# A new order for the first third of a recurrent-attention and gated-MLP kernel

## The chip, the core and the metric

The kernel runs on one core of a Trainium2 chip. The metric is the device time of one execution in microseconds (us). The core has five engines, each with its own queue of instructions that is worked off strictly in order: TensorE (PE, matmuls), VectorE (DVE), ScalarE (ACT), GpSimd (POOL) and SyncE (SP, which issues loads and stores). An instruction that needs another engine's result waits for a semaphore, and everything behind it in its own queue waits too.

## What is computed

The reference has two parts. A gated linear recurrence over 768 time steps, for 4 batches and 8 heads of 48 columns, gives `x`; then a gated MLP with a spatial mix over the time steps:

```python
for t in range(S):
    state = alpha[:, :, t, :, None] * state + einsum('bhd,bhde', k[:, :, t], v[:, :, t])
    y[:, :, t] = einsum('bhd,bhde->bhe', q[:, :, t], state)
x = y.transpose(0, 2, 1, 3).reshape(B, S, H * D)
h = maximum(x @ w_in, 0); u, v = h[..., :512], h[..., 512:]
v_n = (v - mean(v)) / sqrt(var(v) + 1e-6)
v_s = einsum('ts,bsd->btd', w_spatial, v_n) + b_spatial[None, :, None]
out = (u * v_s) @ w_out
```

## The kernel before

The recurrence is done in chunks of 128 steps (six per batch, 24 in all). Within a chunk the running product of alpha is built from logarithms: `ln` (ACT), cumulative sums by matmuls with triangular matrices (`half`, `cum`), then exponentials on ACT: `einv` (e to the minus sum, tile `binv`) and `eexp` (e to the sum, in the PSUM bank). `kt` = k times binv, `qt` = q times the bank; both are transposed on TensorE (`tr_k`, `tr_q`), copied out of PSUM (`ev`), multiplied to scores (`sc`), masked (`ms`, `m`) and multiplied by v (`y`). The state is carried by `upd` (TensorE), `S` and `z` (VectorE, GpSimd) and `sb` (a bf16 copy). `xe` evicts x. The first four chunks are done together (`four_chunks`), and so are the four from chunk 6 on; chunks 4 and 5 are a pair; the rest are single.

The MLP per batch: `v` and `u` project (line 1006, the helper `accumulate`, which all matmuls of the MLP go through), `ve` and `ue` evict with relu, `bn` takes mean and variance, `rs` 1/sqrt, `nm` (line 1085, tile `shift`) minus mean times that, `vn` normalizes. `vn` on ACT reads `shift`; `vn` on VectorE reads the mean itself. `s` mixes over time, `se` adds the bias, `g` gates, `o` projects out, `oe` evicts, `st` stores. The bias `b_spatial` comes by one small load, `b_sp` (line 1206), that GpSimd issues; a matmul with a row of ones, `bb` (line 1033, two halves), spreads it over the partitions, and `be` evicts that to `bsp_bc`. The weights come in float32 into two buffers `raw`, so that each 768 KB load waits for the casts (`cast`) of the load two before it; the spatial weights are then transposed (`wt`, line 1018) and copied out (`we`).

The masks and triangles that are built at the start are `maskq`, `tri`, `triq`, `one`, `ident` and `causal`.

Nothing is scheduled by the machine. A string `PLAN` holds every operation in one list, and `replay` emits them in that order, which fixes the order on each engine. A word of it is an engine's letter and the number of the operation, for TensorE with the PSUM banks that it takes and filling matmuls ahead of it:

```python
P103@6,4,5,7:512#7:424#7   # op 103 on TensorE, banks 6,4,5,7; two filling matmuls into bank 7
...
op, eng = ops[int(word[1:])], LETTERS[word[0]]
...
    warm(int(cols), int(n), kind)
...
op.emit(eng)
```

A filling matmul (`warm`, line 243) multiplies a tile of constants and its result is read by nobody.

Of the kernel before, what the change touches and what calls it, by code (L numbers as in the profile page):

```python
# [37 lines left out]
LETTERS = {"P": "PE", "D": "DVE", "A": "ACT", "G": "POOL", "S": "SP"}  # L38
# [1 line left out]


PLAN = """
D2 D0 D4 D1 G9 G11 G5 G6 D3 S56 S57 S59 S58 A60 S12 S169 S170 A61 S272 S171 D8 P62@0:512#0:512#0:512#0 P66@1 P67 P63
P70@2 P71 P74@3 P75 A68 A64 D79 G82 P91@4,5 P52@6 A69 A72 A76 G7 A78 A92 A84 A65 G88 G87 A73 A77 D85 D90 D81 D93 D53
D83 D80 P103@6,4,5,7:512#7:424#7 P94@0,1 D86 D104 D89 D106 G13 P97@6,2:192#2 D98 A95 P100@3,0 D101 A96 P117@3,6:376#1
P115@4,1 A99 G107 G14 A15 A173 D102 D109 P128@0,2 D119 D118 P174@5 A116 A122 A176 P130@6,4 S16 D132 D131 S172 A135
P175@1 A129 P120@3 P54@2 G110 G105 P136@0,4 A121 A178 A55 G111 G108 P133@6 G181 A180 A134 G184 A179 D112 A177 D138
P123@7,3 P141@2 S20 G276 G277 G278 G17 G19 G18 D124 D125 P151@6 P187@7,4 P126@3 S23 S274 S273 D185 A152 A127 G186 G183
G113 G114 D182 P190@5,6 A189 A192 A142 P144@3 D137 P139@4 D188 D191 A140 G22 G21 D153 D143 P199@6,5 P196@2,7 P162@4
A280 A145 P287@0 A163 P154@1 P160@3 A279 A288 A155 D200 D201 D198 D197 D164 P193@4 A161 P156@7 A157 A165 D194 D146  # L50
P158@5 A159 G195 P202@1,2 P203 S26 A204 A147 D166 P290@4 P37@5,7 D38 P34@3,6 G24 S275 S384 S396 G25 S503 S29 D35
P207@1 D148 D208 D36 A39 A289 P205 P281@7 P40@3,5 A206 A282 A167 G10 D42 P210@2 D149 D150 D41 S385 S386 D168 D209 S398
S397 P284@5 P223@6 P219@3 P221@1 A211 A291 A224 A285 D212 A283 A220 A213 D295 D301 A286 A292 D214 D222 D215 A216
P225@6 P233@2 P217@3 P229@7 P237@0 A218 A28 D298 G297 G27 D304 G294 P226 D227 G300 G303 P43@3,5 D45 P230 P234 D231
D235 A293 A44 P46@4,6 P306@5,1 D308 P238 P49@7,3 D50 D51 A48 A47 A307 P309@2,6 P315@1,4 P312@5,7 P249@3 P250 A310 A316
A314 A296 A311 A299 D313 D317 D239 G236 D251 P338@4,1 P332@7,5 P245@0 P246 G302 G305 D333 D339 G232 P318@7,6,3,2 G240
G228 D340 D319 A507 G33 D334 D321 D247 P253@4 P330@7,1 P254 P241@5 P242 G320 A388 A400 A30 A337 A331 A32 G322 P389@0
D255 P345@7,6 D243 D324 D347 A390 P341@4 A391 P335@5 G31 G325 D394 D327 D346 G393 P401@3 A342 A336 A402 A403 P257@1
A392 S492 S387 A258 P259@4 P356@2 S399 G404 G248 G323 G326 S491 S557 P343@0,7 D405 P351@3,5 P407@1,6 A357 D328 A344
A350 A408 D353 D352 P359@2 G252 G395 P348@7 A349 P354@3 D409 S505 S494 S506 P418@6,1 P413@5,0 D358 S493 S504 S559 S547  # L60
S545 S608 S558 S548 S546 A355 A360 D415 D420 P508@7 P366@3 P410@0 P371@2 P377@1 D411 D414 A260 A509 P375@0 D419 A495
D361 A372 A561 P262@5 P496@6 G244 G329 G406 G256 A367 A376 A510 D368 G412 A497 A498 P416@0 P421@3 A422 G514 G502 G500
D378 D379 D513 G512 A417 P264@2 P267@4 A499 A362 A380 A268 D363 D501 P426@0 P423@1 P435@3 P437@6 D381 A365 A427 A424
P433@4 A434 A438 A382 D263 D436 P269@0 D364 D265 D425 D428 D383 P518@1 P369@4 A511 A270 P562@6 P373@2 A374 A429 A549
# [18 lines left out]
S484 S490 S487 S705 S261 S475 S271 G808 P864@5 D816 P823@3 P819@1 D865 P874@4 D766 D768 A824 S714 A828 A820 A875 A767
A710 D829 P871@3 D830 D831 P887@5 P885@1 P881@4 D876 D872 D873 A877 D878 D879 P913@6 P706@2 A707 P893@3 P883@7 P897@0
A884 A886 A882 A888 P889@2 D880 P894 D895 G896 P890 P898 P905@5 P906 D891 D899 P901@2 P902 G900 P914 P909@0 P910
P917@3 D903 D892 D915 G916 D904 P926@6 P920@2 P918 S708 A927 S928 A921 S922 S711 D911 D907 D908 P923@6 G912 D919
P929@2 A930 D924 S925 S931 P935@3 D936 S937 P932@6 A933 S934 P938@3 D939 S940
"""


# [42 lines left out]
def kernel(  # L133
# [23 lines left out]
    NDS = DH // 128  # L157
# [70 lines left out]
    vn = sb("vn", 2, [128, NT, DH])  # L228
# [37 lines left out]
    ops, made = [], {}  # L266
# [788 lines left out]
    def project_v(b, tt):  # L1055
# [20 lines left out]
        def rs(_):  # L1076
# [3 lines left out]

        op(("rs", b, tt - 1), "ACT", rs,
           [("bn", b, tt - 1), ("bn", b, tt), ("vn", b - 2, tt - 1), ("vn", b - 2, tt), ("zeros", 3)])
        def nm(_):
            for x in (tt - 1, tt):
                nc.vector.tensor_scalar(
                    out=shift[n2][:, x:x + 1], in0=mvs[n2][:, x, 0:1], scalar1=rstd[n2][:, x:x + 1], scalar2=-1.0,
                    op0=ALU.mult, op1=ALU.mult)
# [188 lines left out]
```

## Time and profile before

| | us |
|---|---|
| three runs, median (lowest to highest) | 138.29 (137.82 to 139.09) |
| profiled execution, its own time | 139.19 |
| span of the program in it | 137.4 |
| alpha in use (`ln 0`), first k in use (`kt 0 1` on GpSimd, `kt 0 0` on VectorE) | 5.35, 8.07, 8.40 |
| first attention scores on TensorE (`sc 0`) | 15.44 |
| last matmuls (start, duration of seven) | 133.20, 0.98 |

Times within the profile count from the span's start. A timeline row reads: start, duration, engine, line, operation, what it writes and reads, shape, count, and in brackets the idle time ahead of it with what ended it. A row of groups reads: line, engine, operation, tiles, shape, count, then busy us, mean ns of one, idle time ahead with its releaser. A row of loads reads: tile and source, queue, count, size of one and median us from issue to landing. Consecutive matmuls overlap, so that a matmul's duration is longer than the distance to the next.

### The profile page before, as it was taken

The page shows a single profiled execution, that of the slowest core. Times are in us where ns is not written, and L with a number is a line of the kernel's source. Part 1 is how long each engine was busy: PE and PEld are TensorE (multiplying, and loading weights), DVE is VectorE, ACT ScalarE, POOL GpSimd, SP SyncE. Part 2 cuts the span into 40 slices and gives each one's busy share as a digit, 9 for nine tenths or more (in the row PEclk, how much of TensorE's full clock was granted, in tenths as well). Part 3 has the DMA queues.
Part 4 walks back from the last instruction along what each step waited for, and adds up shares of the span by engine and source line. Part 5 has one row for each costly group of instructions (what it writes and reads, how often), then busy time and mean ns, then how long its engine had stood idle before and what let it go on. Part 6 is the DMA issues. An engine that isn't in the chain of part 4 may idle for free.

```text
span 137.4 us, 5308 instructions
## 1 busy us (share of the span) xinstructions
PE 131.0 (95%) x2122; PEld 79.2 (58%) x2122; DVE 120.8 (88%) x300; ACT 108.0 (79%) x261; POOL 87.2 (63%) x146
## 2 busy tenths in 40 slices
PE   6899998999999999999999999999999999999990
PEld 3365554564646566566657666656566765565560
DVE  6259999979999999999899999997999999974871
ACT  3476998899989889999997989999965796954041
POOL 7365899967399789972079989620799842003560
PEclk9999999999999999999999999999999999999999
DMA  3999999599989796899999797899991497101055
GB/s 83 371 371 382 341 321 347 132 374 383 366 164 261 159 218 127 163 184 192 195 190 209 143 205 147 167 194 226 190 181 23 158 390 257 66 0 57 0 203 203
DMA packets 76473, 28.66 MB, mean 209 GB/s; under 512 B 63008, under 2 KB 74912, under 8 KB 76448
## 3 DMA queue, kind: packets, MB, share of 16 engines
q1 hardware_dynamic: 76416, 28.32, 78.6%
q8 instruction: 16, 0.26, 0.8%
q14 instruction: 9, 0.07, 0.2%
q0 software_dynamic: 32, 0.00, 0.0%
HBM read 23.60 MB, written 4.72 MB: 206 GB/s over the span
## 4 chain that ended last, share of the span: by engine, by line
PE 76%; ACT 6%; DVE 6%; DMA 5%; issue 3%; POOL 2%; SPq 0%; POOLq 0%; ACTq 0%
PE bank L1006 53%; DMA kc<-in_k_dram 5%; PE bank L961 3%; PE bank L945 3%; PE bank L989 3%; PE bank L417 2%; PE bank L855 2%; PE bank L899 2%; PE bank L837 2%; PE bank L933 2%; DVE vn L1097 1%; PE bank L795 1%; PE bank L772 1%; ACT uT L185 1%; DVE w_spT L181 1%
## 5 line engine op out<-in xcount | busy, mean ns | idle before, releaser
L1006 PE MATMUL bank<-w_spT,vn 128*128 128x384 bf16 x192 | 35.8, 327 | 0.3 <-DVE vn L1097 0.3
L190 POOL TENSOR_TENSOR gT<-vs,uT 128x384 bf16<-128x384 f32 x28 | 25.7, 933 | 14.3 <-DVE vs L1153 14.1
L190 POOL TENSOR_TENSOR kt<-kc,binv 128x384 bf16<-128x384 f32 x22 | 20.3, 931 | 20.3 <-ACT binv L909 15.2
L1006 PEld LDWEIGHTS <-vn 128*128 128x128 bf16 x192 | 17.4, 98 | 11.7 <-DVE vn L1097 0.7
L1006 PE MATMUL bank<-w_in,xT 128*128 128x512 bf16 x72 | 19.1, 380 | 0.2 <-ACT xT L179 0.2
L1006 PE MATMUL bank<-xT,w_in 128*128 128x384 bf16 x96 | 18.7, 326 | 0.0
L1006 PE MATMUL bank<-w_out_sb,gT 128*128 128x384 bf16 (+1 forms) x100 | 18.4, 320 | 0.0
L1153 DVE TENSOR_TENSOR vs<-bank,bsp_bc 128x384 f32<-128x384 f32 x31 | 16.3, 550 | 2.4 <-PE bank L1006 2.3
L950 DVE TENSOR_TENSOR ptm<-bank,mask 128x512 bf16<-128x512 f32 x28 | 17.9, 683 | 0.4 <-PE bank L945 0.2
L179 ACT COPY kqT<-bank 128x512 bf16<-128x512 bf16 (+1 forms) x20 | 15.0, 792 | 3.1 <-PE bank L989 1.9
L1068 DVE BATCH_NORM_STATS2 stats<-v_sb 128x6 f32<-128x512 bf16 x24 | 16.4, 682 | 0.2
L185 ACT ACTIVATE v_sb<-bank 128x512 bf16<-128x512 f32 x20 | 11.8, 599 | 1.8 <-PE bank L1006 1.5
L185 ACT ACTIVATE uT<-bank 128x384 bf16<-128x384 f32 x27 | 12.4, 495 | 0.7 <-PE bank L1006 0.6
L1006 PEld LDWEIGHTS <-w_in 128*128 128x128 bf16 x96 | 9.0, 98 | 6.7 <-DVE ptm L950 0.3
L190 DVE TENSOR_TENSOR qt<-qc,bank 128x384 bf16<-128x384 f32 x24 | 12.6, 545 | 0.2 <-DMA qc<-in_q_dram 0.2
L1006 PEld LDWEIGHTS <-gT 128*128 128x128 bf16 x100 | 9.3, 98 | 5.8
L179 ACT CAST xT<-bank 128x384 bf16<-128x384 f32 x23 | 10.4, 482 | 1.8 <-PE bank L417 1.4
L844 DVE TENSOR_TENSOR ptm<-bank,mask 128x512 bf16<-128x512 f32 x16 | 10.4, 684 | 0.0
L1006 PEld LDWEIGHTS <-xT 128*128 128x128 bf16 x72 | 6.2, 97 | 6.2 <-ACT xT L179 1.2
L179 ACT COPY raw_w<-bank 128x384 f32<-128x384 f32 x8 | 3.8, 480 | 7.3 <-PE bank L1006 7.2
L394 DVE TENSOR_TENSOR zs<-bank,state 128x384 f32<-128x384 f32 x16 | 8.8, 549 | 0.5 <-PE bank L933 0.4
L243 PE MATMUL bank<-junk 128*128 128x512 f32 (+3 forms) x14 | 8.0, 700 | 1.1 <-DVE junk L1242 1.1
(162 smaller groups left out, 265.4 us busy)
## 6 DMA issues: line engine op xcount, KB each, us to landing
ac<-in_alpha_dram SPq DMA_DIRECT2D x14, 192.0 KB, 4.4
kc<-in_k_dram SPq DMA_DIRECT2D x14, 192.0 KB, 4.0
qc<-in_q_dram SPq DMA_DIRECT2D x14, 192.0 KB, 4.4
vc<-in_v_dram SPq DMA_DIRECT2D x14, 192.0 KB, 4.1
raw_w<-in_moe_w_spatial_dram SPq DMA_DIRECT2D x3, 768.0 KB, 8.0
out_dram<-o_sb SPq DMA_DIRECT2D x9, 192.0 KB, 2.0
ac<-in_alpha_dram SPq DMA_DIRECT2D x2, 768.0 KB, 6.8
kc<-in_k_dram SPq DMA_DIRECT2D x2, 768.0 KB, 7.6
```

The costliest lines, as they stand in the source:

```text
L179: nc.scalar.copy(out=out, in_=in_)
L185: nc.scalar.activation(out=out, in_=in_, func=AF.Relu)
L190: ENG[eng].tensor_tensor(out=out, in0=in0, in1=in1, op=ALU.mult)
L243: nc.tensor.matmul(out=banks[n][:, 0:cols].rearrange("p (a b) -> p a b", a=4), lhsT=junk, rhs=junk[:, None, 0:cols // 4].to_broadcast([128 ...
L394: lambda _: nc.vector.tensor_tensor(out=zs[i % 3], in0=tp(), in1=state[(i - 1) % 3], op=ALU.add),
L844: nc.vector.tensor_tensor(out=ptm[n2][:, ci, s], in0=banks[sl.bank].rearrange("p (hp t) -> p hp t", hp=HP), in1=mask[:, 3][:, None, :].to_ ...
L945: nc.tensor.matmul(out=pt[s][:, hp, :], lhsT=kT[rows, hp, :], rhs=qT[rows, hp, :], start=True, stop=True)
L950: nc.vector.tensor_tensor(out=ptm[n2][:, ci, s], in0=banks[sl_p[s].bank].rearrange("p (hp t) -> p hp t", hp=HP), in1=mask[:, 2][:, None, : ...
L961: nc.tensor.matmul(out=place(to, 3 * hp + (0, 1, 1, 2)[x]), lhsT=heads(vb, hp, x), rhs=ptm[n2][:, ci, x // 2, hp, :], start=(turn == 0), s ...
L1006: nc.tensor.matmul(out=ps, lhsT=lhsT, rhs=rhs, start=first and n == 0, stop=last and n == len(pairs) - 1)
L1068: nc.vector.bn_stats(out=stats[tt % 2], in_=v_sb[n2][:, tt, :])
L1153: nc.vector.tensor_tensor(out=vs[d], in0=banks[sl.bank][:, 0:TH], in1=bsp_bc[:, th, :], op=ALU.add)
```

## The change

The kernel's `PLAN` is replaced. SyncE's loads and stores keep their order. On the other engines the order is new up to a common operation, from which it is as before: on TensorE the last spatial-mix matmuls of batch 0 (`s 0 0 1 1`), on VectorE `z 7`, on ACT the exponential `einvs 10`, on GpSimd the last cast of w_out. The PSUM banks are dealt anew to the end. Some operations of the first third change engines (before to after):

| from | to | operations |
|---|---|---|
| VectorE | GpSimd | triq, vb 0 0, vb 1 1 |
| VectorE | ACT | be 0, ev_k 1 0, ev_q 1 0, ve 0 4, we 0 1, we 2 0, we 5 0 |
| ACT | VectorE | ev_k 0 0, ev_q 0 0, ev_k 2 1, ev_q 3 0, we 1 1, we 4 0, vn 0 2, vn 0 5 |
| GpSimd | ACT | vb 1 0, sb 0, sb 2, sb 6, and one cast each of w_in 0, w_spatial 2, w_out |
| ACT | GpSimd | vb 3 1, and one cast each of w_in 1, w_spatial 2, two of w_out |
| GpSimd | VectorE | kt 1 1 |

The beginnings of the queues, by names:

| engine | before | after |
|---|---|---|
| GpSimd | maskq, b_sp, tri, ident, kt 0 1, causal, kt 1 1, vb 1 0, cast | maskq, tri, triq, one, ident, causal, kt 0 1, b_sp, vb 1 1, vb 0 0, cast |
| TensorE | half 0 0, half 0 1, cum 0 1, cum 0 0, half 1 0, cum 1 0, half 1 1, cum 1 1, tr_k 0, bb 0, upd 0, tr_q 0, tr_k 1, tr_q 1, sc 0 | half 1 0, half 0 0, half 0 1, cum 0 0, cum 0 1, cum 1 0, half 1 1, cum 1 1, tr_k 0, bb 0, upd 0, tr_k 1, tr_q 0, tr_q 1, sc 0 |
| ACT | ln 0, ln 1, einv 0 1, einv 0 0, eexp 0 1, einv 1 0, einv 1 1, ebc, ev_k 0 0, vb 0 1, eexp 0 0, eexp 1 0, eexp 1 1, ev_q 0 0 | ln 0, ln 1, einv 0 0, einv 0 1, einv 1 0, eexp 0 0, einv 1 1, vb 1 0, vb 0 1, be 0, eexp 1 1, eexp 0 1, ebc, eexp 1 0, ev_k 1 0, ev_k 1 1, ev_q 0 1, ev_q 1 0 |
| VectorE (behind the zeros) | triq, kt 0 0, kt 1 0, vb 1 1, vb 0 0, ev_k 0 1, be 0, qt 0 1, qt 0 0, qt 1 0, S 0, qt 1 1 | kt 0 0, kt 1 0, kt 1 1, ev_k 0 0, ev_k 0 1, qt 1 1, qt 0 1, qt 0 0, S 0, qt 1 0 |

Filling matmuls, in columns: before 512, 512, 512 ahead of the first `half`, 512 and 424 ahead of `upd 0`, 192 ahead of `tr_k 1`, 376 ahead of `sc 0`; after 512, 512, 360 ahead of the first `half`, 416 ahead of `upd 0`, 120 ahead of `tr_q 0`, 384 ahead of `sc 0`.

The second part: `nm` is split into one operation for each of the two tiles, and emits nothing where the `vn` that follows is on VectorE. Before, 24 `shift` instructions are emitted; after, four, since `vn` is on ACT for four tiles (1 1, 1 2, 1 5, 3 0).

```diff
 PLAN = """
-D2 D0 D4 D1 G9 G11 G5 G6 D3 S56 S57 S59 S58 A60 S12 S169 S170 A61 S272 S171 D8 P62@0:512#0:512#0:512#0 P66@1 P67 P63
-P70@2 P71 P74@3 P75 A68 A64 D79 G82 P91@4,5 P52@6 A69 A72 A76 G7 A78 A92 A84 A65 G88 G87 A73 A77 D85 D90 D81 D93 D53
...
+S56 D0 S57 G9 D1 S59 D2 D4 G5 D3 S58 G8 G10 A60 S12 A61 P70@0:512#0:512#0:360#0 G6 P62@1 G7 P66@2 P63 P67 A64 P71 S171
+A68 P74@3 D79 A72 P75 G82 S172 A65 D85 A76 G11 P91@4,5 A87 D88 A84 G90 P52@6 D92 A53 D93 G81 A77 S275
...
 def replay(ops, held, warm, plan):
 
+    for word in plan.split():
+        op = ops[int(re.match("[A-Z]([0-9]+)", word).group(1))]
+        op.eng = LETTERS[word[0]]
     for word in plan.split():
...
-        def nm(_):
-            for x in (tt - 1, tt):
+        for x in (tt - 1, tt):
+            def nm(_, x=x):
+                if made[("vn", b, x)].eng == "DVE":
+                    return
                 nc.vector.tensor_scalar(
                     out=shift[n2][:, x:x + 1], in0=mvs[n2][:, x, 0:1], scalar1=rstd[n2][:, x:x + 1], scalar2=-1.0,
                     op0=ALU.mult, op1=ALU.mult)
 
-        op(("nm", b, tt - 1), "DVE", nm, [("rs", b, tt - 1), ("vn", b - 2, tt - 1), ("vn", b - 2, tt)])
-        for x in (tt - 1, tt):
+            op(("nm", b, x), "DVE", nm, [("rs", b, tt - 1), ("vn", b - 2, x)])
+
             def vnf(e, x=x):
...
-               [("rs", b, tt - 1), ("nm", b, tt - 1)] + [("s", b - 2, d, th, 1) for d in range(NDS) for th in range(2)])
+               [("rs", b, tt - 1), ("nm", b, x)] + [("s", b - 2, d, th, 1) for d in range(NDS) for th in range(2)])
```

In these excerpts G9 is maskq, G5 tri, G8 triq, G10 one, G6 ident, G7 causal, G82 kt 0 1, G11 b_sp, P91 tr_k 0, P52 bb 0, and D53 or A53 be 0.

More of the change, by code (lines that the diff above doesn't have):

```diff
@@ L48 @@
[L48 to L52, printed above, removed]
@@ L83 @@
[L83 to L87, printed above, removed]
+S56 D0 S57 G9 D1 S59 D2 D4 G5 D3 S58 G8 G10 A60 S12 A61 P70@0:512#0:512#0:360#0 G6 P62@1 G7 P66@2 P63 P67 A64 P71 S171
@@ new lines @@
+A68 P74@3 D79 A72 P75 G82 S172 A65 D85 A76 G11 P91@4,5 A87 D88 A84 G90 P52@6 D92 A53 D93 G81 A77 S275
+P103@5,6,4,7:416#7 A69 D89 A78 D83 A73 D80 P97@3,2 D104 A98 D86 S173 A99 G15 P94@1,5:120#1 D106 P100@0,3 A96 D95 A101
+G107 D102 S16 A175 P117@0,3:384#2 G14 P128@1,5 D109 P115@6,2 A105 D119 P177@4 G110 A116 D118 A129 P130@3,6 G108 A135
+D112 P120@0 S174 A180 G13 P123@5,1 D132 A121 P176@7 G186 S20 A181 D131 P141@6 A122 D124 G113 A178 P54@3 P133@2 A182
+D125 G279 P136@5,0 A111 A179 P126@1 D138 A134 G183 D187 A127 P152@2 A142 D184 G114 P189@4,1 D137 G280 A153 P192@6,7
@@ new lines @@
+P144@0 D190 A194 D191 G19 A18 D193 P139@4 D143 G17 A145 P198@6,1 G281 P201@7,2 A55 S23 P155@0 D200 A282 S277 P157@3
+D203 G185 S276 A140 P159@1 G188 D146 A156 P161@4 A158 G22 D199 A283 P195@0 P163@3 D196 A160 A147 D202 P290@6 G197 A164
+P284@0 D154 P204@7,1 A162 G21 A291 P205 D165 D148 D150 P207 G24 S26 P37@4,3 A206 P34@2,5 A208 S278 P209@7 A166 G25
+S389 A292 P212@1 D167 D149 D38 D39 D168 A210 D35 D169 P226@3 D170 A36 D211 S401 P287@7 A213 P40@5,2 A288 P220@4 D214
+A227 P222@1 A41 D42 P293@3 A215 D151 P224@2 A285 D216 D218 D219 A296 P236@5 D217 G297 A221 D225 P237 A289 D304 P240@4
@@ new lines @@
+A294 G300 D301 P232@6 A295 S509 D238 A223 G28 D307 P233 A286 P241 A27 D234 P43@3,1 G303 P309@5,7 D242 S29 P228@6 A44
+D45 G306 A310 D298 P49@1,3 P46@4,2 D311 P229 A50 G305 D51 A48 S390 P312@7,0 D47 G239 P318@3,1 S391 A314 D313 P315@2,4
+P252@5 D320 G302 A319 D316 S403 G308 A405 P253 D230 P335@2,3 G235 A317 D254 P341@6,1 A299 P248@0 D336 G231 A513 D342
+P256@5 A393 G243 D343 P321@2,4,7,6 S402 D337 P244@1 D322 A33 G30 S498 P249 D324 A323 P257 D250 P333@2,3 G325 P245 D258
+A340 P394@0 A334 S392 G32 D246 P348@4,5 A395 P344@3 G31 D327 A396 P338@1 S404 D350 P406@7 G328 A345 P260@2 D399 A339
@@ new lines @@
+S497 G398 A407 D330 P262@3 A408 D349 P359@6 S564 G409 A397 D410 A261 P346@0,4 D331 A360 P354@1,5 G251 S511 P412@2,7
+A347 D356 P362@6 A353 D355 A413 G326 G329 D414 P351@4 S500 G255 P357@1 D361 A352 P423@7,2 A358 S512 P418@4,5 G400
+P514@0 A363 D420 G247 P370@1 A263 S499 D425 A515 P415@5 G332 P375@3 A501 D416 S510 G411 P381@2 A376 D419 G259 A568
+P379@5 D424 A371 P265@4 G417 D364 A380 S566 P502@1 A516 P421@5 D372 A503 S554 P426@7 G520 A504 P267@3 D382 A427 G508
+S552 A422 G506 D383 P270@7 A505 A365 P431@5 S616 D519 G518 A384 D366 D368 P428@2 D507 A271 S565 A369 D385 D387 D266
@@ new lines @@
+P441@6 P443@7 A432 S555 D442 P439@4 A429 D367 P272@6 D268 A440 S553 D430 A444 P524@3 P373@4 A386 P569@7 D433 P377@2
+A517 S628 A273 P445@5 D388 A378 P532@0 P459@6 A434 D446 S630 A556 D525 D435 P455@2 A572 D437 D436 S617 A438 P557@3
+D374 P521@5,1 A570 P460 S567 D523 A571 G573 P447@4 A522 D461 S618 P448 G526 D533 P451@1 A558 D574 S629 A560 P456 G561
+D449 A559 P471@7 D457 A563 S619 P452 G462 D562 P536@2,4 D453 P527@0,5 S736 P576@3,6 D528 G454 P475@1 A577 D529 S724
+P472 G458 D537 P463@0 A620 S727 A632 D538 G534 P476 A578 P579@2 P464 D477 S631 G450 P621@4 D580 P530@3 A622 P539@6
@@ new lines @@
+D473 A531 G581 P583@2,1 D465 A623 P592@7,5 P633@3 A540 G478 D593 P541@0 A634 S726 D626 A575 P467@6 G625 A635 D585
+P479@7 S739 A542 G636 D584 A624 P544@1 D637 S738 G582 P588@2 D594 P468 A545 G627 P639@3,4 S791 A480 D469 G535 P595@1
+D589 A641 P586@6 D640 S725 G590 P642@2 A728 P485@7 D543 A596 G474 S737 P729@3 A587 D643 P650@1,4 A638 P645@5,0 D546
+S793 G644 P482@2 A486 A730 D651 P608@7 A740 G466 A732 D647 P600@1 A609 G591 S779 D646 P597@6 A747 G735 D652 P604@5
+G470 S792 A598 D610 P741@7 P653@4 G733 A744 S780 D599 P648@6 A547 P491@0 A654 S843 D483 D548 D550 A649 P658@4 A795
@@ new lines @@
+D549 D601 A605 P666@6 A492 D551 P751@5 A659 P494@1 S781 D752 A742 P670@4 D660 A611 G745 S794 P655@5 A667 D612 D614
+D615 A671 P602@6 S782 A743 D656 P488@4 A495 D613 A783 S487 P672@1 D657 A489 P606@5 A731 D753 P668@4 S855 A673 D746
+A661 S844 P796@0 P682@7 A607 D662 D664 D663 S845 A603 D665 P678@5 A797 P759@6 A798 P784@1 S846 D760 P683 A785 P679
+D734 A799 P686@6 G788 S856 D680 A786 P694@3 A847 D801 G802 A790 S857 D761 P687 G800 A669 P674@0 D684 A859 S858 P806@4
+D789 A787 P675 G681 D688 P695 P748@1,7 D807 G689 P803@6,5 D696 A749 P702@4 D676 G685 D804 A805 P815@0 P703 D750 G808
@@ new lines @@
+P860@6 P848@1 D704 P754@7,5 A849 G677 P763@3,2 P698@4 D755 A850 A861 G854 D816 P699 A851 G852 D764 P690@7 A862 D700
+P709@0 G863 D756 P691 P706@4 G817 D765 D692 P712@5 A707 D864 A710 G693 P766@7 S708 D853 P757@0 S711 D713 A767 P810@6,4
+G705 S484 P819@1,2 A758 P866@5,7 D812 S269 A809 G697 P768@0 S490 D820 A867 S496 D821 P869@4 G701 P771@1 S493 A762 D811
+S714 A769 P718@2 D870 S264 A868 D770 S481 P822@0 S274 P813@4 A823 D865 P872@7,6 A814 G871 P877@5,3 P721@0 D874 A772
+G818 D879 P835@6 D773 P831@3 A836 P827@1 D878 P824@6 A828 D873 A774 P880@5 D837 A825 P875@7 A832 P833@1 D826 A881
@@ new lines @@
+P829@3 A722 D876 A834 P885@5 S723 D775 D777 A838 D778 P882@1 A830 D839 D841 D840 A886 D842 P899@7 A776 P897@3 D887
+P893@5 A719 D883 P925@0 D884 P715@1 P905@2 A888 A716 P895@6 D889 D891 D890 D892 S717 P909@1 A896 A898 P901@4 A894 P906
+A900 P902 D907 P910 P917@7 D903 G908 D911 P918 P913@4 G912 P914 P926 D915 P921@1 D904 P922 D927 P929@4 D916 G928 D923
+P938@0 D919 P932@1 G924 A939 D920 P930 S940 A933 P935@0 D931 S934 S720 D936 P941@4 S937 P947@0 A942 P944@1 D948 S943
+P950@0 S949 A945 D951 S946 S952
```

34 lines of the change are left out of this document (removed).

## The prediction

> **What bounds the kernel now.** I read the page first, then the busy time of stretches, then the timelines of the first 16 us, because that is where the two orders differ most.
>
> ```profile
> span 137.4 us, 5308 instructions
> ...
> PE 131.0 (95%) x2122; PEld 79.2 (58%) x2122; DVE 120.8 (88%) x300; ACT 108.0 (79%) x261; POOL 87.2 (63%) x146
> ```
>
> TensorE is the engine with the least room. The stretches below begin at the first attention scores (15.44), at the matmul from which TensorE's order is again the old one (47.68), and end with its last matmul.
>
> ```profile
> core 0: us, PE busy (x) PEld busy (x) DVE busy (x) ACT busy (x) POOL busy (x), PEclk, DMA share, GB/s
> 15.44:47.68 32.24, 30.97 (x645) 17.82 (x645) 30.64 (x71) 29.58 (x72) 26.63 (x41) 1.00 0.95 285
> 47.68:134.20 86.52, 86.44 (x1305) 54.23 (x1302) 79.85 (x180) 68.94 (x173) 51.58 (x81) 1.00 0.72 164
> ```
>
> From 47.68 to 134.20 TensorE idles 0.08 us. So whatever the new order wins or loses up to that matmul is handed to the end one for one. In 15.44 to 47.68 its idle time is 32.24 - 30.97 = 1.27 us; that is the most that a better order can take out of this stretch. Before it TensorE waits for the first loads, and filling matmuls sit in the waits:
>
> ```profile
> 9.79 0.33 PE L1033 MATMUL bank<-b_sp_sb,ones_row 1*128 1x384 bf16 x1
> 10.05 1.84 PE L243 MATMUL bank<-junk 128*128 128x512 f32 x4
> 11.82 0.26 PE L795 MATMUL bank<-o_sb,kt 32*128 32x96 bf16 x8
> 12.33 0.78 PE L795 MATMUL bank<-o_sb,kt 32*128 32x96 bf16 x56 [0.24 <-POOL o_sb L181]
> ...
> 14.21 0.41 PE L772 MATMUL bank<-ident,qt 64*128 64x64 bf16 x16
> 14.61 0.90 PE L243 MATMUL bank<-junk 128*128 128x376 f32 x2
> 15.44 0.40 PE L837 MATMUL bank<-kqT 48*128 48x128 bf16 x8
> ```
>
> The reader is to see the first row: the matmul that spreads the bias (bb 0) is early in TensorE's queue and costs nothing at 9.79, because the bias has long landed.
>
> **The change, part by part.** *The bias load moves.* It is the one load that GpSimd issues, so an unchanged order of SyncE's loads does not cover it. GpSimd's rows before:
>
> ```profile
> 1.01 1.36 POOL L339 TENSOR_SCALAR_AFFINE_SELECT mask<-mask 32x128 bf16<-32x128 bf16 x4
> 2.32 0.67 POOL L1206 DMA_DIRECT2D b_sp_sb<-in_moe_b_spatial_dram  x1
> 3.04 0.20 POOL L322 MEMSET le_pair<- 128x128 bf16 x1
> ...
> 4.19 0.20 POOL masks.py:197 MEMSET ident<- 128x128 bf16 x1
> 4.46 0.29 POOL masks.py:199 TENSOR_SCALAR_AFFINE_SELECT ident<-ident 128x128 bf16<-128x128 bf16 x1
> 8.07 0.91 POOL L190 TENSOR_TENSOR kt<-kc,binv 128x384 bf16<-128x384 f32 x1 [3.31 <-ACT binv L741]
> 8.94 1.90 POOL L355 TENSOR_SCALAR_AFFINE_SELECT mask<-mask 64x128 bf16<-64x128 bf16 x4
> ...
> 32.93 0.21 POOL L347 MEMSET le_one<- 128x128 bf16 x1
> ...
> 33.88 0.29 POOL L348 TENSOR_SCALAR_AFFINE_SELECT mask<-mask 128x128 bf16<-128x128 bf16 x1
> ```
>
> ```profile
> 3.84 0.26 DVE L181 COPY le_quad<-le_pair 128x128 bf16<-128x128 bf16 x1 [0.19 <-POOL le_pair L328]
> ...
> 4.63 0.18 DVE L334 MEMSET lt_quad<- 32x16 uint32 x2
> ...
> 11.69 1.48 DVE L190 TENSOR_TENSOR qt<-qc,bank 128x384 bf16<-128x384 f32 x3 [0.20 <-DMA qc<-in_q_dram]
> 13.14 0.56 DVE L190 TENSOR_TENSOR state<-bank,bcq 128x384 f32<-128x384 f32 x1
> 13.61 0.54 DVE L190 TENSOR_TENSOR qt<-qc,bank 128x384 bf16<-128x384 f32 x1
> ```
>
> ```profile
> 7.50 0.87 ACT L741 ACTIVATE binv<-bank 128x384 bf16<-128x384 f32 x2 [0.57 <-PE bank L718]
> ...
> 11.17 1.24 ACT L744 ACTIVATE bank<-bank 128x384 f32<-128x384 f32 x3
> 13.48 1.56 ACT L179 COPY kqT<-bank 128x512 bf16<-128x512 bf16 x3 [1.07 <-PE bank L772]
> ...
> 19.14 0.49 ACT L179 CAST bsp_bc<-bank 128x384 bf16<-128x384 f32 x1
> ```
>
> In the new order GpSimd does, ahead of the bias load: maskq (ends 2.37), tri (3.04 to 4.19, 1.15), triq (0.97 on VectorE, 3.84 to 4.81; on GpSimd no row, I take 1.0), one (32.93 to 34.17, 1.24), ident (0.56), causal (1.90), and the first kt (0.91). The masks end at 2.37 + 1.15 + 1.0 + 1.24 + 0.56 + 1.90 = 8.2. kt 0 1 needs the second exponential binv, which ended at 8.37 and now comes after one more cumulative matmul, so about 8.6; the masks are hidden under that wait, up to a triq of 1.4 us. kt ends at 9.5, and there the bias load is issued instead of at 2.32.
>
> How long it takes to land is the price that decides:
>
> ```profile
> out_dram<-raw_w SPq DMA_DIRECT2D x2, 96.0 KB, 1.7
> b_sp_sb<-in_moe_b_spatial_dram POOLq DMA_DIRECT2D x1, 1.5 KB, 5.3
> ...
> kc<-in_k_dram SPq DMA_DIRECT2D x1, 384.0 KB, 7.8
> ```
>
> The same load took 5.3 us. The ends are 1.7 us, the quickest transfer of the trace (a store, at the end, when the DMA engines are nearly empty), and 7.8 us, a load of 384 KB (kc, pair 2) that SyncE issued in the full stretch around 8.4. I take 5.3, its own row: landing at 14.8. The Trainium skill, "DMA: Bandwidth & Descriptors", section "Anatomy of one DMA — SWDGE (gpsimd) path", gives a GpSimd-issued load about 2.0 us plus bytes / 436e3. By it the bias would land at 11.5 and the sum below would come out near 138.7. This case's row, 5.3, does not agree with it.
>
> *What stands behind it.* TensorE's order keeps bb 0 right after the first transposes, and a queue goes in order. be 0, the eviction of bb 0, moves from VectorE to ACT, ahead of three of the exponentials that qt needs. So both queues stand still until 14.8. From there, by rows:
> - bb 0 0.33, to 15.15. be 0 0.49 on ACT, to 15.7; the two exponentials for the first qts at 1.24 / 3 = 0.41 each, to 16.1 and 16.5.
> - VectorE: three qt from 16.1 at (13.14 - 11.69) / 3 = 0.48 each, to 17.6; state 0.47 (13.14 to 13.61), to 18.05; the fourth qt, to about 18.55. TensorE's update, which the state needs, is done earlier: a filling matmul of 416 columns at the rate of the 376 (0.90), to about 16.1, and 0.26 + 0.78 for the update, to 17.1.
> - TensorE: last transposes 0.41, to 18.95; the filling matmul of 384 columns, kept in the new order, 0.90; first scores at 19.85, where they were at 15.44: +4.4 us. ACT's last copy (1.56 / 3 = 0.52 after 18.95) is done at 19.5, under the filling matmul.
>
> *From the scores to 47.68.* TensorE has the same matmuls in another order, 30.97 us of them. With no idle time it reaches the common order at 19.85 + 30.97 = 50.8 (+3.1); with as much as before at +4.4. I take the middle, **+3.8 us**: VectorE (30.64) and ACT (29.58) are released less late than TensorE by their own sums, so part of the old idle time goes.
>
> *What moves between engines.* Casts, evictions, two of the normalizations and small copies trade places among VectorE, ACT and GpSimd; in that stretch each has between 1.6 and 5.6 us of 32.24 free, so I take nothing, with TensorE's 30.97 as cover. If that cover went, each would cost its own duration.
>
> *Filling matmuls.* Seven become six. Those ahead of the first cumulative sums end before alpha is there in both orders: nothing. After that 512 + 424 + 192 + 376 columns become 416 + 120 + 384, a saving that is in the chain above.
>
> *Shift instructions.*
>
> ```profile
> L1085 DVE TENSOR_SCALAR shift<-mvs,rstd 128x1 f32<-128x1 f32 x24 | 3.9, 206 | 1.0 <-ACT rstd L1079 1.0
> ```
>
> Of 24 only the four whose normalization is on ACT stay: 20 x 0.206 = 4.1 us of VectorE, most of it behind 47.68, where TensorE's 86.44 of 86.52 covers it. I take 0; without that cover, up to 4.1.
>
> *SyncE's loads.* Their order stays, but two wait for casts:
>
> ```profile
> 18.59 6.85 SPq L1048 DMA_DIRECT2D raw_w<-in_moe_w_spatial_dram  x2
> ```
>
> The second of these (its issue ends at 18.59 + 6.85 = 25.44) waits for the buffer that the casts of w_in free. When the chain is 4 us late these casts are late by up to as much, and so is everything behind in SyncE's queue. That cannot be more than the chain's own delay, and is why I don't forecast less than +3.1 in the likeliest case. The banks of the later matmuls are dealt anew; nothing taken.
>
> **Sum.** The profiled execution took 139.19 us (span 137.4): 139.19 + 3.8 = 143.0. It lies 0.9 above the median of the three runs, 138.29; against that, 138.29 + 3.8 = **142.1 us**.
>
> **Rivals.**
> 1. *TensorE falls back to half pace.* It would stand from about 9.9 to 14.8 without work. At the start of the trace the same 512-column passes of the filling matmul are 0.86 apart, later 0.43:
>
> ```profile
> 3.77 0.34 PEld L243 LDWEIGHTS bank<-junk 128*128 128x128 f32 x1 [0.52 <-issue]
> 4.63 0.26 PEld L243 LDWEIGHTS bank<-junk 128*128 128x128 f32 x1 [0.52 <-issue]
> ...
> 10.59 0.19 PEld L243 LDWEIGHTS bank<-junk 128*128 128x128 f32 x1 [0.24 <-issue]
> 11.02 0.19 PEld L243 LDWEIGHTS bank<-junk 128*128 128x128 f32 x1 [0.24 <-issue]
> ```
>
> The slow pace lasted from the start to 4.63, some 3.6 us. As much again after 14.8 costs up to half of it, 1.8 us: 143.9 us. Against it: the granted clock reads 1.00 everywhere, and no row shows TensorE after a long idle time. The Trainium skill, "TensorE: Matmul & The Clock Gate", Part 1, says that TensorE returns to half clock after an idle window of about 3.4 us; by that rule 4.9 us of idle time are enough if they cover such a window.
>
> 2. *The bias lands quickly: not slower.* For it: 1.7 us for the quickest transfer. Landing at 11.2 puts everything above 3.6 earlier: scores at 16.2 (+0.8), the common order at -0.5 to +0.8, and the time at 137.8 to 139.1, say 138.4. Against it: the load's own 5.3 us. It decides when the load lands less than about 2.9 us after issue, since 2.4 us off the +3.8 leaves +1.4, 1%. Were the bias not waited for at all, the scores would come at about 15.4 and the order win its idle time at most: 137.0.
>
> 3. *The bias lands later*, 7.8 us as the loads of that stretch: 2.5 more, 144.6 us.
>
> **How the numbers follow.** +3.8 as worked out 0.45 (its own range, a landing of 4 to 6 us and no or all of the idle time, 140.8 to 143.5); half pace on top 0.25; quick landing 0.25; late landing 0.05. A change of under 1% (1.4 us) is what a measurement of this kernel can't tell from none: slower 0.75, same 0.21, faster 0.04 (both from rival 2). The range from 138.6 to 144.8 leaves out about 0.13 of rival 2 and 0.05 above.
>
> **What would show it.** Right: the bias load starts near 9.5 on GpSimd, TensorE has a gap of about 5 us ahead of bb 0 that the bias load ended, ACT one ahead of bsp_bc, and the first scores stand near 19.9; after the common matmul the stretch to the last one is 86.5 as before. Half pace would show as passes 0.86 apart behind the gap. Wrong: a load issued or landed well before 14.8, or TensorE idle behind the common matmul.

## The result, and the profile after

| | before | after |
|---|---|---|
| median, us (lowest to highest; four runs each) | 138.27 (137.82 to 139.09) | 142.87 (142.74 to 143.03) |
| profiled execution, its own time and span, us | 139.19, 137.4 | 142.99, 141.2 |
| first scores (`sc 0`), us | 15.44 | 20.70 |
| first instruction of the common order on ACT (`einvs 10`), us | 48.51 | 52.32 |

The ratio is 1.0326, with a 95% interval of 1.0276 to 1.0376: slower by 4.6 us between the medians, 3.8 us between the two profiled executions. Ratios here leave disturbed executions out, and medians do not, so the two need not agree to the last tenth. In the changed kernel's code lines stand four lower, and six lower from the split `nm` on (bb 0 is L1037, a filling matmul L247, the scores L841, the bias load L1212).

First the place where the prediction expected the wait: GpSimd's issue of the bias load in the timeline, and that load's row among the DMA issues, whose last number is the time from issue to landing.

```profile
8.93 0.91 POOL L194 TENSOR_TENSOR kt<-kc,binv 128x384 bf16<-128x384 f32 x1 [1.15 <-ACT binv L745]
9.79 0.67 POOL L1212 DMA_DIRECT2D b_sp_sb<-in_moe_b_spatial_dram  x1
...
b_sp_sb<-in_moe_b_spatial_dram POOLq DMA_DIRECT2D x1, 1.5 KB, 4.6
```

Then the timeline of TensorE and of ACT behind it.

```profile
14.47 0.47 PE L1037 MATMUL bank<-b_sp_sb,ones_row 1*128 1x384 bf16 x1 [4.28 <-DMA b_sp_sb<-in_moe_b_spatial_dram]
14.88 1.76 PE L247 MATMUL bank<-junk 128*128 128x416 f32 x2
16.56 1.46 PE L799 MATMUL bank<-o_sb,kt 32*128 32x96 bf16 x64
...
20.70 0.40 PE L841 MATMUL bank<-kqT 48*128 48x128 bf16 x8
```

```profile
14.98 0.48 ACT L183 CAST bsp_bc<-bank 128x384 bf16<-128x384 f32 x1 [4.08 <-PE bank L1037]
15.36 0.87 ACT L748 ACTIVATE bank<-bank 128x384 f32<-128x384 f32 x2
```

The load lands near 14.4, TensorE stands for 4.28 us ahead of bb 0 and ACT for 4.08 ahead of be 0, with the exponentials behind it. The windows of that stretch (length, busy time and count for PE, PEld, which is TensorE's weight loads, DVE, ACT and POOL, then TensorE's granted clock, the DMA share and GB/s) show a second thing:

```profile
10.00:15.00 5.00, 0.72 (x10) 0.29 (x8) 2.50 (x4) 0.92 (x4) 2.03 (x4) 0.67 1.11 366
15.00:20.00 5.00, 4.90 (x117) 3.25 (x118) 3.37 (x8) 3.46 (x9) 0.25 (x1) 0.65 1.12 364
```

The granted clock fell to 0.67 and 0.65, and the filling matmul behind bb 0 took 1.76 us for 416 columns. The loads that depend on casts follow: the issue of the w_spatial loads begins 4.5 us later than before (23.11 against 18.59).

```profile
23.11 6.74 SPq L1052 DMA_DIRECT2D raw_w<-in_moe_w_spatial_dram  x2
```

From the first instruction of the common order to the end the two kernels are alike. One window of each, after first, then before:

```profile
52.32:141.20 88.88, 84.99 (x1286) 53.69 (x1294) 77.97 (x165) 68.53 (x172) 51.19 (x81) 1.00 0.71 164
```

```profile
48.51:137.40 88.89, 85.61 (x1296) 53.62 (x1290) 79.37 (x179) 68.68 (x171) 50.75 (x80) 1.00 0.72 165
```

88.88 and 88.89 us. All of the loss arises ahead of that point. (Of the profiles below, all but one need 88.8 to 89.4 us for this stretch; e3 needed 90.2.)

### The profile page after: what moved, and what is told of

It reads as the page before. It is cut to its first block, busy times and chain, and to the rows that moved or that the text cites. A ratio compares the mean times of both kernels' runs of the same rounds, so it can differ in the third digit from the quotient of the medians.

```text
span 141.2 us, 5260 instructions
## 1 busy us (share of the span) xinstructions
PE 129.6 (92%) x2106; PEld 79.6 (56%) x2120; DVE 118.1 (84%) x274; ACT 107.5 (76%) x262; POOL 86.2 (61%) x151
## 4 chain that ended last, share of the span: by engine, by line
PE 81%; DMA 7%; ACT 5%; issue 3%; DVE 1%; POOL 1%; POOLq 0%; ACTq 0%
PE bank L1010 56%; DMA ac<-in_alpha_dram 3%; DMA b_sp_sb<-in_moe_b_spatial_dram 3%; PE bank L949 3%; PE bank L965 3%; PE bank L993 3%; PE bank L421 2%; PE bank L903 2%; PE bank L937 1%; PE bank L247 1%; PE bank L859 1%; PE bank L722 1%; PE bank L1022 1%; PE bank L841 1%; ACT vb L183 1%
## 5 line engine op out<-in xcount | busy, mean ns | idle before, releaser
L194 POOL TENSOR_TENSOR kt<-kc,binv 128x384 bf16<-128x384 f32 x21 | 19.5, 937 | 20.5 <-ACT binv L913 15.3
L1010 PE MATMUL bank<-w_in,xT 128*128 128x512 bf16 x58 | 17.4, 380 | 1.6 <-ACT xT L183 0.6
L183 ACT COPY kqT<-bank 128x512 bf16<-128x512 bf16 (+1 forms) x18 | 14.0, 806 | 3.3 <-PE bank L993 1.8
L189 ACT ACTIVATE v_sb<-bank 128x512 bf16<-128x512 f32 x21 | 12.4, 598 | 1.8 <-PE bank L1010 1.5
L1103 DVE TENSOR_SCALAR vn<-v_sb,mvs,rstd 128x512 bf16<-128x512 bf16 x20 | 8.0, 417 | 1.2 <-ACT rstd L1083 1.0
```

Source lines behind the costliest of these rows:

```text
L183: nc.scalar.copy(out=out, in_=in_)
L189: nc.scalar.activation(out=out, in_=in_, func=AF.Relu)
L194: ENG[eng].tensor_tensor(out=out, in0=in0, in1=in1, op=ALU.mult)
L1010: nc.tensor.matmul(out=ps, lhsT=lhsT, rhs=rhs, start=first and n == 0, stop=last and n == len(pairs) - 1)
L1103: nc.vector.tensor_scalar(out=vn[n2][:, x, :], in0=v_sb[n2][:, x, :], scalar1=mvs[n2][:, x, 0:1], scalar2=rstd[n2][:, x:x + 1], op0=ALU.su ...
```

## The experiments

Theory 1: the late bias load, for which TensorE and ACT stand still, is the loss, and the rest of the change is about neutral. Theory 2: the rest of the new order (engines swapped, banks dealt anew) costs it. Theory 3: the pause matters through the half pace that it leaves on TensorE. In the table the times are medians, each ratio is against the kernel before in the same series, and `sc 0` and `einvs 10` are starts in the one execution that was profiled. e2, e8 and e9 start from the kernel before, the others from the changed kernel. The diffs show only the words around an edit; the rest of their lines is left out.

| kernel | median us | ratio (95% interval) | sc 0 | einvs 10 |
|---|---|---|---|---|
| e1 bias load first | 139.00 | 1.0089 (1.0057 to 1.0120) | 15.37 | 48.50 |
| e2 kernel before, load late | 144.02 | 1.0420 (1.0383 to 1.0457) | 20.52 | 52.66 |
| e3 load late, readers later | 139.33 | 1.0062 (1.0025 to 1.0100) | 16.88 | 48.24 |
| e4 fills in the wait | 141.35 | 1.0250 (1.0209 to 1.0292) | 19.23 | 52.04 |
| e5 load one place earlier | 141.01 | 1.0184 (1.0143 to 1.0226) | 19.53 | 50.55 |
| e6 load and readers later | 139.82 | 1.0076 (1.0040 to 1.0112) | 15.38 | 47.52 |
| e7 e1 with all shifts | 141.55 | 1.0245 (1.0203 to 1.0287) | 15.52 | 50.45 |
| e8 before, second profile | 138.03 | one run | 15.66 | 47.36 |
| e9 before, shifts left out | 138.99 | 1.0052 (1.0018 to 1.0086) | 15.44 | 48.30 |
| e10 changed, all shifts | 145.26 | 1.0488 (1.0430 to 1.0546) | 21.45 | 54.41 |
| e11 e1 with eleven fills | 138.44 | 1.0019 (0.9988 to 1.0049) | 15.46 | 48.32 |
| e12 e1 with 22 fills | 145.13 | 1.0484 (1.0425 to 1.0543) | 21.70 | 54.41 |

### e1: the bias load first

```diff
-S56 D0 S57 G9 D1 S59 D2 D4 G5
+S56 D0 S57 G9 G11 D1 S59 D2 D4 G5
-D85 A76 G11 P91@4,5
+D85 A76 P91@4,5
```

> The changed kernel with one edit: GpSimd issues the bias load second, right behind maskq, as the kernel before does. Theory 1 (the late bias load, for which TensorE and ScalarE stand still, is the whole loss and the rest of the new order is about neutral): the first scores return from 20.7 us to 15 to 16, no idle of more than 1 us on TensorE ahead of bb 0, the clock row has no 6 or 5, and the time is 137.3 to 138.9, within 1% of the kernel before. Theory 2 (the rest of the new order costs: engines swapped, banks dealt anew): over 140.5, most of the 4.6 us between the medians stays. Theory 3 (the pause only matters through the half pace behind it): the same as theory 1 here.

Measured: 139.00 us, 3.9 us under the changed kernel, and no pause:

```profile
9.89 0.33 PE L1037 MATMUL bank<-b_sp_sb,ones_row 1*128 1x384 bf16 x1
10.15 0.97 PE L247 MATMUL bank<-junk 128*128 128x416 f32 x2
11.52 0.86 PE L799 MATMUL bank<-o_sb,kt 32*128 32x96 bf16 x64 [0.40 <-DVE kqT L185]
...
15.37 0.40 PE L841 MATMUL bank<-kqT 48*128 48x128 bf16 x8
```

The same filling matmul takes 0.97 instead of 1.76 and `upd` 0.86 instead of 1.46. Theory 2 falls as the main cause. 0.9% over the kernel before remains, 0.1 us over the forecast 138.9.

### e2: the kernel before, with the load late

```diff
-G9 G11 G5 G6
+G9 G5 G6
-G82 P91@4,5
+G82 G11 P91@4,5
```

> The kernel before with one edit: the bias load is issued behind kt 0 1 on GpSimd, as in the changed kernel. Theory 1: the old order loses as much as the new one: issue near 9, landing 4.6 to 5.3 us later, bb 0 near 14, first scores near 19.5 to 20.5, time 141 to 143. Theory 2: about 138.3, since the old order is otherwise untouched.

Measured: 144.02 us, 5.9 over before, so the one move makes a loss of that size in the old order too, and more than the 3 to 5 us that were expected.

```profile
13.69 0.32 PE L1033 MATMUL bank<-b_sp_sb,ones_row 1*128 1x384 bf16 x1 [3.75 <-DMA b_sp_sb<-in_moe_b_spatial_dram]
13.94 3.21 PE L243 MATMUL bank<-junk 128*128 128x512 f32 x4
```

The four passes of filling took 1.84 us in the kernel before and 3.21 here: the old order has more columns of filling behind the pause, nearly all at the slow pace.

### e3 and e6: the load late, and its readers too

e3 moves bb 0 and be 0 back; e6 also moves the load behind the two casts of v.

```diff
-G90 P52@6 D92 A53 D93 G81 A77
+G90 D92 D93 G81 A77
-P144@0 D190 A194 D191 G19 A18 D193
+P144@0 P52@5 D190 A194 D191 G19 A18 A53 D193
```

```diff
-D85 A76 G11 P91@4,5
+D85 A76 P91@4,5
-D93 G81 A77
+D93 G81 G11 A77
```

> The changed kernel, the bias load as late as it is there, but its two readers moved back: bb 0 on TensorE behind v 0 1, be 0 on ScalarE six words later, so that nothing early waits for the load. Theory 1: the pause is gone though the load is late: first scores at 15 to 16, time 137.3 to 138.9. Theory 2: over 140.5. If the load itself disturbed something other than its readers (the loads of SyncE beside it, GpSimd's queue), the time would stay over 140.5 too, with the first scores early.

> The run with the two readers moved back (bb 0 and be 0), and the bias load two operations later still on GpSimd, behind the two casts of v. There the third kt on VectorE took 1.66 us with the load's issue and the two casts beside it, where it took 0.85 beside the casts alone in the run with the load first. If the issue next to it is what holds VectorE: the third kt takes 0.85, TensorE's idle time ahead of upd falls from 1.48 to about 0.4, the clock row shows no 6, first scores at 15.2 to 15.5 instead of 16.88, time 138.0 to 139.0. If the casts or the missing bb 0 are the reason: kt stays at 1.66, first scores near 16.9, time 139.3.

Measured: e3 139.33 us, so the late load costs through its readers, though the scores came at 16.88 only and the time is 0.4 over the forecast 138.9. VectorE's second and third `kt` tell why; their row in the timeline of the changed kernel (e3 has the same 2.63) and in that of e6:

```profile
9.21 2.63 DVE L194 TENSOR_TENSOR kt<-kc,binv 128x384 bf16<-128x384 f32 x2 [0.21 <-ACT binv L745]
```

```profile
8.97 1.83 DVE L194 TENSOR_TENSOR kt<-kc,binv 128x384 bf16<-128x384 f32 x2 [0.21 <-ACT binv L745]
```

With the load's issue and the casts beside it the third `kt` alone took 1.66 us; with the issue gone it took 0.85 (e1, e5, e6). In e6 the scores came at 15.38 and the clock row is whole, as expected, though the load took 6.2 us there. Its median, 139.82, is outside the expected 138.0 to 139.0: its runs lie between 138.16 and 140.91, and the profile is one of the fastest. So the 1.5 us at the scores cannot be found again in the medians of e3 and e6. Nor is e3's profile the rule: it took 140.14 us with a mean granted clock of 0.988, and eight of its ten executions had 0.996 or more.

### e4: filling matmuls in the wait

```diff
-P52@6
+P52@6:512#6:512#6:512#6:512#6
```

> The changed kernel with four filling matmuls of 512 columns (eight passes, some 3.8 us at the pace of the kernel before) ahead of bb 0, so that TensorE is busy while it waits. Theory 1: the wait decides, the half pace behind it is worth 0.8 to 0.9 us (fill 416 in 0.97 instead of 1.76): first scores 19.8 to 20.0, clock row 9 throughout, time 141.9 to 142.5. Theory 3 (the half pace is the larger part of the loss): under 140.5. If the filling matmuls outlast the landing, bb 0 starts later than 14.5 and nothing is won.

Measured: 141.35 us, 1.5 under the changed kernel.

```profile
10.00 3.70 PE L247 MATMUL bank<-junk 128*128 128x512 f32 x8
14.33 0.32 PE L1037 MATMUL bank<-b_sp_sb,ones_row 1*128 1x384 bf16 x1 [0.63 <-DMA b_sp_sb<-in_moe_b_spatial_dram]
14.58 0.96 PE L247 MATMUL bank<-junk 128*128 128x416 f32 x2
15.48 0.86 PE L799 MATMUL bank<-o_sb,kt 32*128 32x96 bf16 x64
```

The load is as late as ever, but what stands behind it runs at full pace: 0.80 us from the filling matmul, 0.60 from `upd`, 0.15 from bb 0, and 0.14 from an earlier landing, together 1.69; the scores came 1.47 earlier, since the transposes behind `upd` now wait 0.25 us for VectorE. I had counted the filling matmul alone (0.8 to 0.9), so the expected 141.9 to 142.5 and 19.8 to 20.0 were missed. By the medians and the scores the half pace is 1.3 to 1.5 of the 4.6 us, less than theory 3 wants and more than theory 1 gave it. The profiled execution, at 142.70 the slowest of four, does not show the gain at the end: it is only 0.28 us ahead at einvs 10, with a stop of 1.36 us on the way that e11 and e12 look into.

### e5: the load one place earlier

```diff
-D79 A72 P75 G82
+D79 A72 P75 G11 G82
-D85 A76 G11 P91@4,5
+D85 A76 P91@4,5
```

> The changed kernel with the bias load one place earlier on GpSimd, ahead of kt 0 1 instead of behind it. GpSimd sat idle 1.15 us ahead of kt 0 1, so kt 0 1 is not later, and the issue moves from 9.79 to about 7.8. Theory 1 (the time follows the landing): landing 4.6 us later at 12.4, up to 13.1 by the 5.3 of the kernel before; bb 0 1.4 to 2.1 us earlier than at 14.47, first scores 18.6 to 19.3, time 140.8 to 141.5. If the half pace goes away with the shorter idle time, 1.4 us less again: 139.4 to 140.1. If the landing is set by the loads in front of it and not by the issue, nothing changes: 142.9.

Measured: 141.01 us, inside the 140.8 to 141.5 of theory 1; the scores, at 19.53, are 0.2 later than it allows.

```profile
12.70 0.47 PE L1037 MATMUL bank<-b_sp_sb,ones_row 1*128 1x384 bf16 x1 [2.63 <-DMA b_sp_sb<-in_moe_b_spatial_dram]
13.10 1.75 PE L247 MATMUL bank<-junk 128*128 128x416 f32 x2
```

The load was issued at 7.7 and landed 4.9 us later. The pause of 2.63 us was enough for the half pace: the filling matmul took 1.75, and the granted clock of the windows from 10 to 15 and 15 to 20 us is 0.72 and 0.60.

### e7, e9 and e10: the second part of the change alone

e7 is e1, and e10 the changed kernel, with the early return taken out (the diff), so that 24 shift instructions are emitted; e9 is the kernel before with a shift only where `vn` is on ACT (6 of 24).

```diff
-                if made[("vn", b, x)].eng == "DVE":
-                    return
```

> The run with the bias load first, and all 24 shift instructions emitted as in the kernel before (20 more on VectorE, 0.2 us each). If they are hidden behind TensorE, as taken for the removal: the same time as that run, 139.0 within 0.4. If VectorE bounds some stage: up to 4 us of work more, 139.5 or over.

> The changed kernel with all 24 shift instructions emitted (the second part of the change undone, the new order and the late load kept). If the two parts add up: 2.0 to 2.6 us over the changed kernel, 144.9 to 145.5. If the removal is covered by TensorE, as the prediction took it: 142.9. If the pause at the bias load leaves slack that hides them: between.

> The kernel before with the second part of the change alone: a shift instruction is emitted only where the vn behind it is on ScalarE (6 instead of 24). With the bias load first, emitting all of them cost 2.5 us in the new order, where a shift waited 0.93 us for rstd on VectorE and two copies of w_spT and a vn came late for TensorE (0.44, 0.31, 0.63). In the second profile of the kernel before TensorE stands idle 0.25 us in all from 19 to 41 us. If a shift costs only where it stands in front of something that TensorE waits for: 137.6 to 138.2, no difference. If VectorE bounds the stage in any order: 135.5 to 136.5.

Measured: e7 141.55, 2.55 over e1; e10 145.26, 2.4 over the changed kernel; e9 138.99, no gain, and above both expectations. In the new order the shifts are not covered. One row of VectorE and the waits of TensorE in e7:

```profile
32.76 0.22 DVE L1089 TENSOR_SCALAR shift<-mvs,rstd 128x1 f32<-128x1 f32 x1 [0.93 <-ACT rstd L1083]
```

```profile
25.11 0.35 PE L859 MATMUL bank<-ptm,vb 128*32 128x128 bf16 x12 [1.12 <-issue]
33.88 0.65 PE L1010 MATMUL bank<-xT,w_in 128*128 128x384 bf16 x3 [0.44 <-DVE w_spT L185]
36.76 0.65 PE L1010 MATMUL bank<-xT,w_in 128*128 128x384 bf16 x3 [0.31 <-DVE w_spT L185]
...
38.69 2.45 PE L1010 MATMUL bank<-w_spT,vn 128*128 128x384 bf16 x14 [0.63 <-DVE vn L1101]
```

The first row of TensorE is a stop like one in e1 (0.95 there; see e11 and e12); the waits below it are not in e1. A shift waits for rstd with copies of w_spT and a `vn` queued behind it, for which TensorE then waits. The six shifts of the first batch take 1.05 us by themselves (0.30 for two, 0.22, 0.20, 0.33 for two), less than they cost. e7 is 1.95 behind e1 at einvs 10 and 2.1 at the end: it is the first batch's shifts that cost, and the later ones are hidden, as the prediction has it. Two effects had cancelled: the new order without the second part is 3.5 us slower than before even with the load first (e7), and the second part gives 2.4 to 2.55 of it back.

### e8: the kernel before, again

> The kernel before, unchanged, for a second profile: the first one is of the slowest of its executions (139.19, where the median is 138.2). Expected: about 138.2, span about 136.4, and the microsecond between the two profiles in a stretch where loads arrive late, not in the opening; first scores at 15.4 again.

Measured: 138.03, span 136.2; scores at 15.66, einvs 10 at 47.36, 1.15 earlier than in the first profile. Against this profile the changed kernel loses 5.0 us at the scores, 5.0 at einvs 10 and 5.0 at the end: by this pair of executions nothing is given back. The seeming recovery from +5.3 to +3.8 belonged to the first profile.

### e11 and e12: TensorE's stops

e1's profile has idle time of TensorE that ended on "issue" (it waited for nothing that the profile shows), in the middle of an operation. Two kernels, both e1 with one more edit, move TensorE's instruction stream without changing the work that counts:

```diff
-P70@0:512#0:512#0:360#0
+P70@0:128#0:128#0:128#0:128#0:128#0:128#0:128#0:128#0:128#0:128#0:128#0
```

e12 has 22 of `:64#0` there.

> The run with the bias load first, and the three filling matmuls ahead of the first half cut into eleven of 128 columns: 1,408 columns where there were 1,384, all ahead of alpha's arrival, but 16 weight loads (32 instructions) more on TensorE. With the load first TensorE stopped 1.18 us in the middle of y (line 859), behind its 351st weight load; the earlier trace with eight weight loads more stopped behind the 351st too, there in the transposes of line 540. If a stop belongs to the place in TensorE's instruction stream (instructions are fetched in blocks): it stands behind the 351st weight load again, which is now in the transposes, 16 loads earlier in the program, and none in the middle of that y. If y waits for data or a bank: the stop stays in y, behind the 367th. Time: the same 139.0 within 1.0, since the stop can get longer or shorter.

> The same with 22 filling matmuls of 64 columns (1,408 columns, 38 weight loads more than with the load first). By the place in the instruction stream: the 351st load is now the second of the transposes of line 540, so a stop stands there or, if the block has arrived by then, nowhere; none in y. By data or a bank: in y, behind the 389th. Time: 138.0 to 140.0; under 138.0 if the stop is gone altogether and nothing takes its place.

Measured: the stop of e1, that of e4 and that of e11, one row of each timeline.

```profile
24.69 0.35 PE L859 MATMUL bank<-ptm,vb 128*32 128x128 bf16 x12 [0.95 <-issue]
```

```profile
27.89 0.20 PE L540 MATMUL bank<-ident,qt 64*128 64x64 bf16 x1 [1.36 <-issue]
```

```profile
24.05 0.32 PE L540 MATMUL bank<-ident,qt 64*128 64x64 bf16 x9 [0.90 <-issue]
```

All three stand behind the 351st weight load counted from the start, in whatever operation that is; e11's is in the transposes, as the place in the stream requires. So y waits for no data. Two stops in one trace (e1: 351st and 479th, the second of 0.41 us) are 128 weight loads apart, 256 instructions with their matmuls. e11 took 138.44 us, not to be told from before. e12's expectation of the time failed for another reason; the fills at the start of e12, then of e11, and a later row of e12:

```profile
1.05 9.65 PE L247 MATMUL bank<-junk 128*128 128x64 f32 x44 [1.05 <-DVE junk L1248]
```

```profile
1.05 4.78 PE L247 MATMUL bank<-junk 128*128 128x128 f32 x22 [1.05 <-DVE junk L1248]
```

```profile
40.28 1.15 PE L1010 MATMUL bank<-xT,w_in 128*128 128x384 bf16 x6 [1.45 <-issue]
```

44 passes of 64 columns took 9.65 us, 0.22 each, where 22 of 128 took 4.78, also 0.22 each: at the start of the program half the columns cost as much, and the opening was 5 us late. The first matmuls behind them were slow as well (three cumulative sums in 1.17 us, 0.65 in e11). e12 showed no stop in y; its one long stop, 1.45 us, stands behind the 607th weight load, 2 x 128 behind the 351st.

## Why the prediction was right

- **The wait (right).** Issue at 9.79 for the forecast 9.5, landing 4.6 us later for 5.3, the bias at 14.4 for 14.8. TensorE's pause was 4.28 and ACT's 4.08 for "about 5". e1 and e2 show that the late load makes the loss: 3.9 us taken out of the new order, 5.9 put into the old one.
- **The first scores (the wait right, two terms too small and the path behind the wait another).** 20.70 for 19.85. The terms that were mis-sized are the filling matmul (1.76 for 0.90) and the update (1.46 for 0.26 + 0.78): both ran at half pace, which the likeliest case left out. The prediction had the update done at 17.1, half a microsecond before VectorE asks for it, and let the path run over VectorE. The update ended at 18.02, and VectorE stood for it:

```profile
18.11 0.56 DVE L194 TENSOR_TENSOR state<-bank,bcq 128x384 f32<-128x384 f32 x1 [0.75 <-ACT bank L748]
```

  The profile names ACT, whose last row into that bank ended at 17.33; that it was the update is inferred from its end at 18.02, and in e2 the profile names the update for the same wait. TensorE itself has no gap over 0.1 us between bb 0 and the scores, so the path lay there. Rival 1, with its bound of 1.8 us, happened; e4 puts it at 1.3 to 1.5. The Trainium skill, "TensorE: Matmul & The Clock Gate", Part 1, has TensorE at half clock after an idle window of about 3.4 us; the trace agrees for 4.28 us of idle time, and e5 shows it after 2.63 already.
- **From the scores to the common order (the number fitted for a wrong reason).** The prediction let 0.6 of 4.4 us be given back, since VectorE and ACT are released less late. By e8 nothing is given back; what looked so is that the first profile of the kernel before was an execution some 1 us slow in that stretch. So 143.0 for the measured 142.99 is luck: the 0.85 us that was missing at the scores and the 0.85 us more that seemed to be given back cancel. Against the median the sum was 142.1, and 142.87 was measured.
- **The new order and the second part (the step that failed).** "I take 0" for engines and shifts stood on TensorE as the cover. e7 and e10 put the shifts of the new order at 2.4 to 2.55 us, ahead of the common point, where VectorE feeds TensorE directly; the order with all shifts costs 3.5 (e7), about 1 more. The sum of both is near the 0 that was taken, by cancelling. The bound of 4.1 was too high by its own row, which has 3.9 us of busy time for all 24; and the six shifts ahead of the common order cost more than their own duration, since one of them waits. Rival 2 has 137.0 at best for a bias that is not waited for: e1 has its first scores at 15.37, where 15.4 was expected, and took 139.00, so the new order wins nothing.
- **Behind the common order (right).** 88.88 us for 88.89.
- **SyncE's loads (right).** w_spatial's issue is 4.5 us late, no more than the chain.
- **Rivals 2 and 3.** The load took 4.6 to 4.9 us from issue to landing wherever it was issued between 7.7 and 10.0, and 6.2 when issued at 11.1 (e6). The quick landing, by which the change would not have been slower, did not come; nor did 7.8. Issued at 2.3, in e1, it took 5.3.

What stays open: how much of e1's 0.8 us is the stops. e1's profile has 0.95 and 0.41 us of them and e8's none, and e11, where the second is absent, has nearly no loss left; but one profile of each kernel can't say how often they come. Why e3, e6 and e9 spread over 2 us was not found, and the new order was not taken apart into its swaps of engines and its sequence.

## What to carry over

A small load counts from where it is issued, not from its size: look for who stands in order behind its reader on every engine, and move either the load forward or the reader back: both took out most of the loss here (e1, e3). A pause on TensorE can cost more than its own length when the work behind it runs at half pace, so fill it if it cannot be removed (e4). An instruction that costs nothing in one order can cost in another: whether a stage covers it is read from what the engine that carries it feeds next, not from the share of busy time.

## What was not expected of the hardware

- **TensorE stops at fixed places in its instruction stream.** The page of e1 has one row for the instruction queue (packets, MB, share):

```profile
q8 instruction: 16, 0.26, 0.8%
```

  Its packets are of 16,384 bytes. In e1 one packet starts at 22.34 and TensorE goes on at 24.69; in e4 25.42 and 27.88, in e11 21.86 and 24.04, in before 21.89 and 24.14: 2.2 to 2.5 us each time. Where that moment came before TensorE reached the place (e8: 21.13 and 23.56; e3: 22.18 and 24.91) there was no stop. That TensorE waits for this packet is inferred from these times and from e11; nothing in the trace names it. The Trainium skill, "Runtime: NRT & Kernel Launch", section "Instruction fetch mechanics", has instructions fetched in 16 KiB blocks of 256, mostly hidden; the size and the 128 weight loads between two stops agree, but here 0.2 to 1.5 us were not hidden.
- **A load's issue on GpSimd beside VectorE.** A `kt` took 0.56 us on VectorE alone, 1.05 beside a `kt` on GpSimd, 0.85 beside casts there, and 1.66 with the bias load's issue and casts. In e2 a `kt` beside the issue and a select took 0.64, as it did beside selects alone in the kernel before, so that the issue by itself does not explain it. The casts beside the 1.66 took 0.52 each, those beside the 0.85 took 0.80 and 0.83: in the one case VectorE alone was held up, in the other both. What decides between the two was not tried. The Trainium skill, "GPSIMD Engine Reference", section "Specifications", has GpSimd share its SBUF interfaces with VectorE, with contention where a VectorE instruction has two SBUF inputs; the 1.05 and 0.85 agree.
- **Shorter pauses can lower the clock too.** After 0.63 us (e4) the pace was full, and after 2.63 and more it was close to half (1.75 and 1.76 us for a filling matmul of 0.97). After 1.48, in e3's profile, the update took 1.18 us instead of 0.86, at a granted clock of 0.79 and 0.87 in the windows from 10 to 15 and 15 to 20 us:

```profile
12.49 1.18 PE L799 MATMUL bank<-o_sb,kt 32*128 32x96 bf16 x64 [1.48 <-DVE kqT L185]
```

  But only two of e3's ten executions show so low a mean clock (0.988), where all four of the changed kernel have 0.976. After 1.48 us it falls at times; whether the length of the pause alone decides, no run here tells.
